# Full-array matmuls outside the projections, and projections as eight 64-by-32 tiles, in an attention and long-convolution kernel on one core

## The chip, the cores and the metric

The kernel runs on one core of a Trainium2 chip. The metric is device time in microseconds (us) of one execution. TensorE (PE) multiplies, VectorE (DVE) and ScalarE (ACT) empty PE's results out of PSUM, GpSimd (POOL) works on SBUF alone and issues the loads, SyncE (SP) issues the stores.

## What is computed

Two softmax attentions per batch and head, then a gated long convolution with its output projection:

```python
# q, k, v: (8, 8, 576, 64); p: (8, 8, 32, 64)
p_packed = sm_attn(p, k, v)              # 32 packed queries against 576 positions
out = sm_attn(q, p_packed, p_packed)     # 576 positions against the 32 packed rows
x = out.transpose(0, 2, 1, 3).reshape(8, 576, 512)
proj = x @ w_proj                        # (8, 576, 1536) -> x1, x2, x3
x2_conv = irfft(rfft(x2, axis=1) * rfft(filter_fft, axis=0), n=576, axis=1)
result = (x1 * x2_conv * x3) @ w_out     # (8, 576, 512)
```

## The kernel before

Each batch passes through four stages, each a Python generator that issues a small piece of work and then yields the time that its author counted for the piece.

- `front(b)`: transposes of k (`kTp`), p (`pTp`, function `pack`) and q (`qTp`, and `qTtp` for the last 64 positions, function `q_tail`), the first attention (`s1`, `pv`, `z1`), the transpose `ppT` of its result into the tile `ppk`, and the second scores (`score2`), which leave the softmax weights `a2n`.
- `turn(b)`: the packed rows times `w_proj` (`qp`, into `qm`), then `a2n` times the forward Fourier matrix `wc` (`fp`, `fpt`) and the transposes of `a2n` (`a2tp`).
- `middle(b)`: `spectrum` (the spectrum `f`, times the filter into `tt`, sums on POOL into `gm`) and `gate` (the products `x1` and `x3`, into `w`).
- `back(b)`: `inverse` (inverse transform `x2`, times `w` into `y`) and `project_out` (`o`, scaled into `os`, stored).

The function `together` merges four stages of four different batches: it takes each time the stage that is least far along by yielded time over its total (`STAGES`). So one round of the main loop, in full with `back(b-3)`, `middle(b-2)`, `turn(b-1)` and `front(b)`, is full for b = 4 to 7. Each engine runs its own instructions in the order that results. All 576 positions are handled as four tiles of 128 and one of 64.

PSUM is two rings of buffers: three called `pa` (all of `front` and `turn`) and five called `pm` (`middle`, `back`). A new tile waits for the reader of the tile three (or five) places earlier in its ring.

A matmul whose stationary operand has 64 columns, or whose contraction has 64 rows, runs in a smaller tiling of the PE array; rows of the profile show it as 128\*64 or 64\*128 (rows \* columns). Before, these are: the four transposes of `pack` and of `ppT` (line 218, 306), `q_tail` (257), the tail of `score2` (325), both matmuls of each projection (354), the fifth matmul of each `fp` and `fpt` group (368, 375), the fifth transpose of each `a2tp` (384), and the tail of `project_out` (460). All others are in the full tiling.

Of the kernel before, what the change touches and what calls it, by code (L numbers as in the profile page):

```python
# [11 lines left out]
FP32 = mybir.dt.float32  # L12
# [34 lines left out]
def _constants(S):  # L47
# [31 lines left out]
def kernel(  # L79
# [42 lines left out]
    wc = const.tile([P, 5, 640], FP16, tag="wc", name="wc")  # L122
# [3 lines left out]
    hri = const.tile([P, 2, 2, DM], FP32, tag="hri", name="hri")  # L126
    hni = const.tile([P, 2, DM], FP32, tag="hni", name="hni")
# [4 lines left out]
    rings = [const.tile([P, H, 2 * NPK], FP16, tag=f"ppk{r}", name=f"ppk{r}") for r in range(NR)]  # L132
    filt = [sb.tile([P, DM], FP32, tag="os", name=f"filt{i}", bufs=5) for i in range(5)]
# [6 lines left out]
    def load(b):  # L140
# [5 lines left out]
        qt = ld.tile([64, H, D], FP16, tag="qt", name=f"qt_b{b}")  # L146
# [14 lines left out]
    nc.scalar.dma_start(wc[0:64, 4, :], d_wc.ap()[0:64, 4, :])  # L161
# [11 lines left out]
    for r in range(NR):  # L173
        nc.vector.memset(pks[r][:], 0.0)
        nc.vector.memset(rings[r][:], 0.0)


    def prologue_filter():
# [5 lines left out]
        dst = [hri[:, 0, 0, :], hri[:, 1, 0, :], hri[:, 0, 1, :], hri[:, 1, 1, :], htail[:]]  # L184
# [15 lines left out]
    def front(b):  # L200
# [8 lines left out]
        qTt = sb.tile([P, H // 2, 64], FP16, tag="qTt", name=f"qTt_b{b}")  # L209
# [44 lines left out]
        def q_tail():  # L254
            tp = pst(f"qTtp_b{b}", [P, H // 2, 64], FP16)
            for g in range(H // 2):
                nc.tensor.transpose(tp[:, g, :], qt[:, 2 * g:2 * g + 2, :], ident[0:64, 0:64])
            nc.vector.tensor_copy(out=qTt[:], in_=tp[:])
# [44 lines left out]
        pT = pst(f"ppT_b{b}", [P, 2, P], FP16)  # L303
        for t in range(2):
            for u in range(2):
                nc.tensor.transpose(pT[u * D:(u + 1) * D, t, :], ppn[:, t, :], ident[:])
        for u in range(2):
            nc.vector.tensor_copy(out=R[u * D:(u + 1) * D, :, (1 - u) * NPK:(2 - u) * NPK],
                                  in_=pT[u * D:(u + 1) * D].rearrange("p t (h j) -> p (t h) j", j=NPK))
# [251 lines left out]
```

## Time and profile before

| | |
|---|---|
| median of 3 runs | 259.2 us (258.7 to 260.14) |
| the profiled execution | 259.07 us, of which 257.3 us are from its first to its last instruction |
| PE, DVE, ACT, POOL busy | 233.8, 157.8, 135.1, 136.2 us |
| mean granted PE clock | 0.979 of full |

Busy time is the time in which an engine has at least one instruction under way. On PE, matmuls overlap, so that its use is better read from the distance between starts.

### The profile page before, as it was taken

The page shows a single profiled execution, that of the slowest core. Times are in us where ns is not written, and L with a number is a line of the kernel's source. Part 1 is how long each engine was busy: PE and PEld are TensorE (multiplying, and loading weights), DVE is VectorE, ACT ScalarE, POOL GpSimd, SP SyncE. Part 2 cuts the span into 40 slices and gives each one's busy share as a digit, 9 for nine tenths or more (in the row PEclk, how much of TensorE's full clock was granted, in tenths as well). Part 3 has the DMA queues.
Part 4 walks back from the last instruction along what each step waited for, and adds up shares of the span by engine and source line. Part 5 has one row for each costly group of instructions (what it writes and reads, how often), then busy time and mean ns, then how long its engine had stood idle before and what let it go on. Part 6 is the DMA issues. An engine that isn't in the chain of part 4 may idle for free.

```text
span 257.3 us, 5269 instructions
## 1 busy us (share of the span) xinstructions
PE 233.8 (91%) x2034; PEld 137.9 (54%) x2034; DVE 157.8 (61%) x382; ACT 135.1 (53%) x267; POOL 136.2 (53%) x128
## 2 busy tenths in 40 slices
PE   0949879977998999999999999999999999999983
PEld 0327527643565566565655565566656553565541
DVE  2241445894129759954795479556966596659560
ACT  2234575460845855664656565755575465442513
POOL 8215274679114859548844784347432843463640
PEclk9998999995899999999999999999999999999999
DMA  5999999991199493978666857112002200230314
GB/s 154 247 224 202 202 198 202 195 196 16 6 175 222 66 130 46 109 119 134 135 80 79 127 150 108 43 41 89 17 3 80 83 23 1 82 104 38 129 40 167
DMA packets 36522, 28.70 MB, mean 112 GB/s; under 512 B 8080, under 2 KB 31184, under 8 KB 36496
## 3 DMA queue, kind: packets, MB, share of 16 engines
q0 software_dynamic: 29504, 16.52, 48.5%
q1 hardware_dynamic: 6336, 11.10, 12.6%
q10 hardware_dynamic: 656, 0.74, 1.0%
q8 instruction: 16, 0.26, 0.4%
q14 instruction: 10, 0.08, 0.1%
HBM read 35.42 MB, written 9.44 MB: 174 GB/s over the span
## 4 chain that ended last, share of the span: by engine, by line
PE 77%; DMA 6%; POOL 6%; ACT 5%; issue 3%; DVE 2%; POOLq 1%; ACTq 0%; DVEq 0%
PE o_b L460 12%; PE x_b L451 9%; PE fp_b L368 7%; PE x_b L424 6%; PE f_b L401 6%; DMA kn_b<-in_k_dram 6%; PE qp_b L354 6%; PE x_b L429 5%; PE pv_b L286 4%; PE s_b L238 4%; PE kTp_b L227 4%; PE qTp_b L248 3%; PE hp L190 3%; PE a2tp_b L384 2%; POOL tt_b L411 2%
## 5 line engine op out<-in xcount | busy, mean ns | idle before, releaser
L411 POOL TENSOR_TENSOR tt_b<-tt_b,tt_b 128x1024 f32<-128x1024 f32 x16 | 37.7, 2354 | 44.0 <-DVE tt_b L409 43.9
L460 PE MATMUL o_b<-wout,y_b 128*128 128x512 f16 (+1 forms) x160 | 41.3, 380 | 0.2 <-ACT x1s_b L426 0.2
L356 ACT CAST qm_b<-qp_b 128x512 f16<-128x512 f32 x48 | 27.8, 594 | 25.1 <-PE qp_b L354 24.6
L431 DVE TENSOR_TENSOR w_b<-x1s_b,x_b 128x288 f32<-128x288 f32 x64 | 28.3, 451 | 20.1 <-ACT x1s_b L426 19.5
L451 PE MATMUL x_b<-ac,gm_b 128*128 128x288 f16 x192 | 37.0, 302 | 3.8 <-POOL gm_b L415 1.7
L463 ACT ACTIVATE os_b<-o_b 128x512 f32<-128x512 f32 (+1 forms) x40 | 23.9, 597 | 30.2 <-PE o_b L460 29.9
L409 DVE TENSOR_TENSOR tt_b<-f_b,hri 128x512 f32<-128x512 f32 x48 | 31.4, 680 | 7.5 <-PE f_b L401 7.5
L426 ACT COPY x1s_b<-x_b 128x288 f32<-128x288 f32 x64 | 25.2, 397 | 16.7 <-PE x_b L424 16.3
L453 DVE SCALAR_TENSOR_TENSOR y_b<-w_b,x_b 128x288 f16<-128x288 f32 x64 | 27.3, 447 | 6.7 <-PE x_b L451 6.5
L333 POOL TENSOR_TENSOR a2n_b<-e_b,zr_b 128x512 f16<-128x512 f16 (+1 forms) x24 | 21.3, 903 | 13.2 <-DVE zr_b L332 7.7
L424 PE MATMUL x_b<-a2t_b,qm_b 128*128 128x288 f16 x128 | 27.0, 288 | 0.2 <-ACT x1s_b L426 0.2
L429 PE MATMUL x_b<-a2t_b,qm_b 128*128 128x288 f16 x128 | 26.7, 286 | 0.0
L451 PEld LDWEIGHTS <-gm_b 128*128 128x128 f16 x192 | 17.0, 102 | 15.0 <-issue 5.0
L401 PE MATMUL f_b<-qm_b,fa_b 128*128 128x512 f16 x80 | 24.3, 379 | 0.2 <-ACT x1s_b L426 0.2
L368 PE MATMUL fp_b<-wc,a2n_b 128*128 128x512 f16 (+1 forms) x80 | 21.9, 381 | 1.1 <-POOL a2n_b L333 1.1
L460 PEld LDWEIGHTS <-y_b 128*128 128x128 f16 (+1 forms) x160 | 14.1, 100 | 15.6 <-issue 4.1
L354 PE MATMUL qp_b<-wp,ppk 128*64 128x512 f16 x96 | 20.6, 405 | 0.9 <-ACT e_b L328 0.5
L240 ACT ACTIVATE e_b<-s_b 96x384 f16<-96x384 f32 x32 | 15.6, 488 | 9.3 <-PE s_b L238 8.5
L227 PE MATMUL kTp_b<-ident,kn_b 96*128 96x96 f16 x192 | 14.0, 210 | 5.2 <-DMA kn_b<-in_k_dram 3.6
L369 ACT CAST fa_b<-fp_b 128x512 f16<-128x512 f32 x16 | 9.4, 586 | 14.8 <-PE fp_b L368 14.8
L227 PEld LDWEIGHTS <-kn_b 96*128 96x128 f16 x192 | 11.1, 101 | 9.4 <-issue 4.2
L238 PEld LDWEIGHTS <-kT_b 128*96 128x96 f16 x192 | 13.7, 131 | 3.9 <-issue 0.9
(70 smaller groups left out, 380.0 us busy)
## 6 DMA issues: line engine op xcount, KB each, us to landing
out_dram<-os_b SPq DMA_DIRECT2D x32, 256.0 KB, 2.3
kn_b<-in_k_dram POOLq DMA_DIRECT2D x8, 576.0 KB, 9.7
vn_b<-in_v_dram POOLq DMA_DIRECT2D x8, 576.0 KB, 9.6
qn_b<-in_q_dram POOLq DMA_DIRECT2D x8, 512.0 KB, 10.5
wp<-in_moe_w_proj_dram POOLq DMA_DIRECT2D x3, 512.0 KB, 20.1
filt<-in_moe_filter_fft_dram SPq DMA_DIRECT2D x4, 256.0 KB, 8.4
out_dram<-os_b SPq DMA_DIRECT2D x16, 64.0 KB, 2.8
wc<-c_wc ACTq DMA_DIRECT2D x4, 160.0 KB, 6.6
```

Source lines behind the costliest of these rows:

```text
L227: nc.tensor.transpose(tp[:, hh, ii, :], kn[:, 2 * g + hh, ts(ii, P)], ident[0:KP, 0:KP])
L354: mark["project"] = nc.tensor.matmul(qp[u * D:(u + 1) * D, :], Rd[:, g, NPK:3 * NPK], wp[:, g, ts(c, DM)], start=True, stop=True)
L356: nc.scalar.copy(out=qm[:, t, ts(c, DM)], in_=qp[:])
L368: nc.tensor.matmul(fp[:], a2n[0:n, i, ts(t, P)], wc[0:n, i, 0:DM], start=(i == 0), stop=(i == 4))
L401: nc.tensor.matmul(f[:], fa[:, t, ts(m, P)], qm[:, t, ts(1, DM)], start=(t == 0), stop=(t == 1))
L409: nc.vector.tensor_tensor(out=x[:, j, :], in0=f[:], in1=h, op=ALU.mult)
L411: nc.gpsimd.tensor_tensor(out=x[:], in0=tt[r][:], in1=x[:], op=ALU.add)
L424: nc.tensor.matmul(x1[:], qm[:, t, ts(m, P)], a2t[:, t, cols], start=(t == 0), stop=(t == 1))
L429: nc.tensor.matmul(x3[:], qm[:, t, ds(2 * DM + m * P, P)], a2t[:, t, cols], start=(t == 0), stop=(t == 1))
L431: nc.vector.tensor_tensor(out=w[:, m, e, :], in0=x1s[:], in1=x3[:], op=ALU.mult)
L451: nc.tensor.matmul(x2[:], gm[:, 4 if j == 2 else 2 * e + j, ts(m, P)], ac[:, j, cols], start=(j == 0), stop=(j == 2))
L460: nc.tensor.matmul(o[0:n, :], y[:, m, COL0[i]:COL0[i] + n], wout[:, m, :], start=(m == 0), stop=(m == ND - 1))
```

## The change

Every matmul outside the projections is brought to the full tiling (the filter's prologue apart, with its ten 64-row matmuls). The two 128-row halves of p and of the packed result are transposed by one matmul in place of four, and spread by four copies of 64x128, two on ACT and two on DVE, in place of two of 64x256 on DVE. The last 64 positions are packed by head parity: head 2g in rows 0 to 63, head 2g+1 in rows 64 to 127 (tiles `a2c`, `e2c`, `qTm`). The fifth block of `wc` gets a second copy in rows 64 to 127, so that 320 KB of it are loaded in place of 80. A projection of one third of `w_proj` becomes eight matmuls of 64 rows and 32 columns with two PSUM tiles, in one piece of `turn` (three pieces, before six). The filter's three parts lie side by side in `h3`, so that one DVE instruction of 1024 elements takes the place of two of 512. Two totals in `STAGES` and some yields are other numbers.

```diff
-    wc = np.zeros((P, 5, 640), dtype=np.float16)
+    wc = np.zeros((P, 6, 640), dtype=np.float16)
     for i in range(5):
         wc[0:TILE_SZ[i], i, :] = _f16(fwd[:, TILE_T[i]].T)
+    wc[64:128, 5, :] = wc[0:64, 4, :]
...
         def pack():
-            pp = pst(f"pTp_b{b}", [P, 2, P], FP16)
+            pp = pst(f"pTp_b{b}", [P, P], FP16)
+            nc.tensor.transpose(pp[:], pn[:], ident[:])
             for t in range(2):
-                for u in range(2):
-                    nc.tensor.transpose(pp[u * D:(u + 1) * D, t, :], pn[:, t, :], ident[:])
-            for u in range(2):
-                nc.vector.tensor_copy(out=pk[u * D:(u + 1) * D, :, u * NPK:(u + 1) * NPK],
-                                      in_=pp[u * D:(u + 1) * D].rearrange("p t (h j) -> p (t h) j", j=NPK))
+                for a in range(2):
+                    cp = nc.scalar.copy if t == a else nc.vector.tensor_copy
+                    cp(out=pk[a * D:(a + 1) * D, 4 * t:4 * t + 4, a * NPK:(a + 1) * NPK],
+                       in_=pp[t * D:(t + 1) * D, :].rearrange("p (h j) -> p h j", j=NPK))
...
+        def score2_tail():
+            sp = pst(f"s2t_b{b}", [P, P])
+            for gg in range(2):
+                for u in range(2):
+                    nc.tensor.matmul(sp[:, ts(gg, 2 * NPK)], qTm[:, gg, u, :], Rd[:, 2 * u + gg, NPK:3 * NPK],
+                                     start=(u == 0), stop=(u == 1))
+            normal(sp[:], e2c[:], a2c[:], zs[:, 4, 0:4], zr[:, 4, 0:4])
...
-        def project(c, t):
-            qp = pst(f"qp_b{b}", [P, DM])
+        def project(c):
+            qp = [pst(f"qp_b{b}", [P, DM]) for u in range(2)]
+            for g in range(H // 2):
+                for u in range(2):
+                    mark["project"] = nc.tensor.matmul(
+                        qp[u][g * NPK:(g + 1) * NPK, :], R[u * D:(u + 1) * D, 4 * u + g, (1 - u) * NPK:(2 - u) * NPK],
+                        wp[u * D:(u + 1) * D, g, ts(c, DM)], start=True, stop=True)
             for u in range(2):
-                g = 2 * t + u
-                mark["project"] = nc.tensor.matmul(qp[u * D:(u + 1) * D, :], Rd[:, g, NPK:3 * NPK],
-                                                   wp[:, g, ts(c, DM)], start=True, stop=True)
-            nc.scalar.copy(out=qm[:, t, ts(c, DM)], in_=qp[:])
+                nc.scalar.copy(out=qm[:, u, ts(c, DM)], in_=qp[u][:])
...
+        def forward(o, t, cols):
+            for i in range(4):
+                nc.tensor.matmul(o, a2n[:, i, ts(t, P)], wc[:, i, cols], start=(i == 0), stop=False)
+            nc.tensor.matmul(o, a2c[:], wc[:, 4 + t, cols], start=False, stop=True)
...
-            for j in range(2):
-                h = hri[:, r, j, :] if m < 2 else (hni[:, r, :] if j == 0 else hri[:, r, 0, :])
-                nc.vector.tensor_tensor(out=x[:, j, :], in0=f[:], in1=h, op=ALU.mult)
+            h = h3[:, r, 1:3, :] if m < 2 else h3[:, r, 0:2, :]
+            nc.vector.tensor_tensor(out=x[:], in0=f[:].unsqueeze(1).broadcast_to([P, 2, DM]), in1=h, op=ALU.mult)
...
-                nc.tensor.matmul(o[0:n, :], y[:, m, COL0[i]:COL0[i] + n], wout[:, m, :],
+                nc.tensor.matmul(o[:], y[:, m, ds(COL0[i], P)], wout[:, m, :],
...
-    STAGES = ((back, 7200.0), (middle, 9400.0), (turn, 3900.0), (front, 5800.0))
+    STAGES = ((back, 7200.0), (middle, 9400.0), (turn, 4300.0), (front, 5700.0))
```

The written order of each engine's instructions shows what moves. Counted there, PE changes its tiling 241 times before and 66 times after; 17 of the 24 projections run as eight matmuls in a row, three of these 17 directly after one another at the start, and the other seven are cut in two by matmuls in the full tiling.

On PE, in the rows of a full round where the projections begin, one pair of projection matmuls before (`qp` the projection, `x` the inverse transform, `kTp` the transpose of k; between the last two rows shown stands a second load and matmul of the pair):

```order
L451 MATMUL x_b_1989<-ac,gm_b_1488 128x288
L354 LDWEIGHTS ppk_80
L354 MATMUL qp_b_1976<-wp,ppk_80 64x512
L451 LDWEIGHTS gm_b_1488
L424 LDWEIGHTS qm_b_1496
```

and after, where two PSUM tiles alternate through eight loads and eight matmuls (each of the two repeats four times):

```order
L422 MATMUL f_b_1970<-qm_b_1518,fa_b_1680 128x512
L373 LDWEIGHTS ppk_79
L373 MATMUL qp_b_1976<-wp,ppk_79 32x512
L373 MATMUL qp_b_1977<-wp,ppk_79 32x512
L232 LDWEIGHTS kn_b_1496
```

So two pieces of `turn` with one PSUM tile each became one piece with two.

On ACT, in the stretch from the projections' first copies on (`qm` is the copy of a projection, `x1s` of a gate product, `kT` of a transposed k, `e` an exponential of scores), before:

```order
L328 ACTIVATE e_b_1848<-s_b_1906 64x256
L356 CAST qm_b_1947<-qp_b_1948 128x512
L356 CAST qm_b_1947<-qp_b_1976 128x512
L426 COPY x1s_b_1997<-x_b_1994 128x288
L232 COPY kT_b_1987<-kTp_b_1980 128x576
L356 CAST qm_b_1947<-qp_b_2003 128x512
L240 ACTIVATE e_b_1952<-s_b_2007 96x2x6x32
```

and after, with the copies of the second attention's packed rows (`ppk`) ahead of them:

```order
L318 COPY ppk_79<-ppT_b_1863 64x2x2x32
L483 ACTIVATE os_b_1893<-o_b_1888 64x512
L446 COPY x1s_b_1907<-x_b_1904 128x288
L331 ACTIVATE e_b_1869<-s_b_1875 128x512
L331 ACTIVATE e2c_b_1870<-s2t_b_1942 128x128
L377 CAST qm_b_1975<-qp_b_1976 128x512
L377 CAST qm_b_1975<-qp_b_1977 128x512
L225 COPY pk_77<-pTp_b_1999 64x4x32
L446 COPY x1s_b_2039<-x_b_2036 128x288
L237 COPY kT_b_2017<-kTp_b_2010 128x576
L377 CAST qm_b_1975<-qp_b_2024 128x512
L245 ACTIVATE e_b_1988<-s_b_2045 96x2x6x32
```

Four copies (two of `ppk`, two of `pk`) are new on ACT; the second one of `ppk` stands behind `os`, the copy of the output tail, and the second one of `pk` behind `kT`.

On DVE, from the row sums of the second softmax to the first `y` of the inverse transform's second half, before:

```order
L329 TENSOR_REDUCE zs_b_1850<-e_b_1848 128x16
L332 RECIPROCAL zr_b_1851<-zs_b_1850 128x16
L385 COPY a2t_b_1656<-a2tp_b_1899 128x576
L329 TENSOR_REDUCE zs_b_1850<-e_b_1848 64x8
L385 COPY a2t_b_1656<-a2tp_b_1915 128x576
L453 SCALAR_TENSOR_TENSOR y_b_1933<-w_b_1489,x_b_1934 128x288
L409 TENSOR_TENSOR tt_b_1944<-f_b_1941,hri 128x512 x2
L230 COPY kT_b_1962<-kTp_b_1955 128x576
L220 COPY pk_78<-pTp_b_1964 64x8x32 x2
L453 SCALAR_TENSOR_TENSOR y_b_1933<-w_b_1489,x_b_1971 128x288
```

and after:

```order
L406 COPY a2t_b_1681<-a2tp_b_1897 128x576
L333 TENSOR_REDUCE zs_b_1873<-e_b_1869 128x16
L406 COPY a2t_b_1681<-a2tp_b_1922 128x576
L333 TENSOR_REDUCE zs_b_1873<-e2c_b_1870 128x4
L473 SCALAR_TENSOR_TENSOR y_b_1962<-w_b_1512,x_b_1963 128x288
L429 TENSOR_TENSOR tt_b_1973<-f_b_1970,h_72 128x1024
L235 COPY kT_b_1997<-kTp_b_1990 128x576
L225 COPY pk_77<-pTp_b_1999 64x4x32 x2
L473 SCALAR_TENSOR_TENSOR y_b_1962<-w_b_1512,x_b_2005 128x288
```

The sequence is the same but for the first copy of `a2t`, which moved ahead of the first row sum, and for the sizes: one `tt` of 1024 elements, a narrower tail sum, and `pk` copies of half the width.

## Rows read from the trace of the kernel before

**Rows 1.** The page's busy times: us, share of the span, instructions.

```profile
PE 233.8 (91%) x2034; PEld 137.9 (54%) x2034; DVE 157.8 (61%) x382; ACT 135.1 (53%) x267; POOL 136.2 (53%) x128
```

**Rows 2.** Chain that ended last, rounds b=4 and b=7: start, us, what.

```profile
110.33 0.97 PE o_b L460 x4
...
190.62 0.97 PE o_b L460 x4
```

**Rows 3.** Timeline of PE, 149 to 156 us: start, us, line, tiling, moving shape, count.

```profile
149.10 0.41 PE L424 MATMUL x_b<-a2t_b,qm_b 128*128 128x288 f16 x2
149.34 0.41 PE L429 MATMUL x_b<-a2t_b,qm_b 128*128 128x288 f16 x2
149.68 0.29 PE L257 MATMUL qTtp_b<-ident,qt_b 64*128 64x64 f16 x4
149.90 0.42 PE L424 MATMUL x_b<-a2t_b,qm_b 128*128 128x288 f16 x2
...
150.50 0.30 PE L306 MATMUL ppT_b<-ident,ppn_b 128*64 128x128 f16 x4
150.63 1.03 PE L460 MATMUL o_b<-wout,y_b 128*64 128x512 f16 x4
...
152.09 0.40 PE L322 MATMUL s_b<-ppk,qT_b 128*128 128x64 f16 x8
152.32 0.77 PE L375 MATMUL fpt_b<-wc,a2n_b 128*128 128x64 f16 x10
```

**Rows 4.** Timeline of PE, 128 to 137.5 us, the stretch of the projections.

```profile
130.38 0.30 PE L451 MATMUL x_b<-ac,gm_b 128*128 128x288 f16 x1
130.60 0.41 PE L354 MATMUL qp_b<-wp,ppk 128*64 128x512 f16 x2
130.94 0.42 PE L451 MATMUL x_b<-ac,gm_b 128*128 128x288 f16 x2
...
132.46 0.59 PE L401 MATMUL f_b<-qm_b,fa_b 128*128 128x512 f16 x2
...
134.06 0.41 PE L354 MATMUL qp_b<-wp,ppk 128*64 128x512 f16 x2
...
137.03 0.82 PE L460 MATMUL o_b<-wout,y_b 128*128 128x512 f16 x3
```

**Rows 5.** Timelines of DVE, 123 to 129 and 127 to 156 us.

```profile
126.45 0.69 DVE L329 TENSOR_REDUCE zs_b<-e_b 128x16 f32<-128x512 f16 x1 [0.16 <-ACT e_b L328]
...
131.99 0.82 DVE L453 SCALAR_TENSOR_TENSOR y_b<-w_b,x_b 128x288 f16<-128x288 f32 x2
...
135.02 0.44 DVE L453 SCALAR_TENSOR_TENSOR y_b<-w_b,x_b 128x288 f16<-128x288 f32 x1
```

**Rows 6.** Timeline of ACT, 127 to 156 us.

```profile
133.43 0.59 ACT L356 CAST qm_b<-qp_b 128x512 f16<-128x512 f32 x1 [0.65 <-PE qp_b L354]
...
151.69 0.59 ACT L463 ACTIVATE os_b<-o_b 64x512 f32<-64x512 f32 x1 [0.94 <-PE o_b L460]
```

**Rows 7.** Groups by shape: count, busy us, mean ns of one, idle before.

```profile
L409 DVE TENSOR_TENSOR tt_b<-f_b,hri 128x512 f32<-128x512 f32 x48 | 31.4, 680 | 7.5 <-PE f_b L401 7.5
L431 DVE TENSOR_TENSOR w_b<-x1s_b,x_b 128x288 f32<-128x288 f32 x64 | 28.3, 451 | 20.1 <-ACT x1s_b L426 19.5 <-PE s_b L322 0.2
L385 DVE COPY a2t_b<-a2tp_b 128x576 f16<-128x576 f16 x16 | 6.6, 416 | 0.5 <-PE a2tp_b L384 0.5
L220 DVE COPY pk<-pTp_b 64x256 f16<-64x256 f16 x16 | 4.5, 283 | 0.1
L329 DVE TENSOR_REDUCE zs_b<-e_b 64x8 f32<-64x256 f16 x8 | 3.1, 387 | 0.0
L377 ACT CAST fa_b<-fpt_b 128x256 f16<-128x256 f32 x8 | 3.0, 373 | 0.7 <-PE fpt_b L375 0.7
L354 PEld LDWEIGHTS <-ppk 128*64 128x64 f16 x96 | 6.0, 107 | 11.9 <-issue 9.8 <-DVE tt_b L409 0.2
```

**Rows 8.** Busy time by stretch; the last three columns are PE clock, DMA share, GB/s.

```profile
10.00:20.00 10.00, 6.40 (x40) 3.01 (x39) 3.45 (x7) 2.57 (x5) 1.71 (x3) 0.90 1.34 224
```

More of the change, by code (lines that the diff above doesn't have):

```diff
@@ L121 @@
     ident = const.tile([P, P], FP16, tag="ident", name="ident")
-    wc = const.tile([P, 5, 640], FP16, tag="wc", name="wc")
+    wc = const.tile([P, 6, 640], FP16, tag="wc", name="wc")
     ac = const.tile([P, NI, S], FP16, tag="ac", name="ac")
@@ L132 @@
     rings = [const.tile([P, H, 2 * NPK], FP16, tag=f"ppk{r}", name=f"ppk{r}") for r in range(NR)]
+    qTms = [const.tile([P, 2, 2, P], FP16, tag=f"qTm{r}", name=f"qTm{r}") for r in range(2)]
     filt = [sb.tile([P, DM], FP32, tag="os", name=f"filt{i}", bufs=5) for i in range(5)]
@@ L175 @@
         nc.vector.memset(rings[r][:], 0.0)
+    for r in range(2):
+        nc.vector.memset(qTms[r][:], 0.0)
     def prologue_filter():
@@ L254, in q_tail @@
         def q_tail():
[L255 to L258, printed above, removed]
+            tp = pst(f"qTtp_b{b}", [P, 2, P], FP16)
+            for gg in range(2):
+                nc.tensor.transpose(tp[:, gg, :], qt[:, 2 * gg:2 * gg + 2, :], ident[:])
+            for u in range(2):
+                c = slice(u * 64, (u + 1) * 64)
+                nc.vector.tensor_copy(out=qTm[:, :, u, c].rearrange("p g (e r) -> p g e r", e=2),
+                                      in_=tp[:, :, c].rearrange("p g (r e) -> p g e r", e=2))
         k_turn(0)
@@ L302, in front @@
         yield 150
-        pT = pst(f"ppT_b{b}", [P, 2, P], FP16)
+        pT = pst(f"ppT_b{b}", [P, P], FP16)
+        nc.tensor.transpose(pT[:], ppn[:], ident[:])
+        Rv = R.rearrange("p (u t g) c -> p u t g c", u=2, t=2)
         for t in range(2):
[L305 to L309, printed above, removed]
@@ L310, in front @@
-        yield 230
-        e2 = sb.tile([P, 5, HJ], FP16, tag="e2", name=f"e2_b{b}")
-        a2n = sb.tile([P, 5, HJ], FP16, tag="a2n", name=f"a2n_b{b}")
+            for a in range(2):
+                cp = nc.scalar.copy if t == a else nc.vector.tensor_copy
+                cp(out=Rv[a * D:(a + 1) * D, :, t, :, (1 - a) * NPK:(2 - a) * NPK],
+                   in_=pT[t * D:(t + 1) * D, :].rearrange("p (g u j) -> p u g j", g=2, u=2))
+        yield 60
+        e2 = sb.tile([P, 4, HJ], FP16, tag="e2", name=f"e2_b{b}")
@@ L316, in score2 @@
         def score2(ii):
-            n = P if ii < 2 else 64
-            w = 2 if ii < 2 else 1
             sp = pst(f"s2_b{b}", [P, 2, HJ])
-            if ii < 2:
-                for h in range(H):
-                    nc.tensor.matmul(sp[:, :, ts(h, NPK)], qT[:, h, ii, :], R[:, h, :], start=True, stop=True)
-            else:
-                for g in range(H // 2):
-                    nc.tensor.matmul(sp[0:64, 0, ts(g, 2 * NPK)], qTt[:, g, :], Rd[:, g, NPK:3 * NPK],
-                                     start=True, stop=True)
@@ L513 @@
     first = turn(0)
-    some(first, 6)
+    some(first, 3)
     def ahead():
```

80 lines of the change are left out of this document (42 added, 38 removed).

## Prediction

> **What bounds the kernel now.** I read four views in this order. The busy times come first [rows 1]: PE is busy for 91% of the span, DVE for 61%, ACT and POOL for 53%. That makes PE the candidate, but its matmuls overlap, so the next question is what the chain that ended last goes through. In the middle of the run it lies on PE, and the same four matmuls of the output projection come back at 110.33 and, three rounds later, at 190.62 [rows 2]: 80.29 / 3 = 26.76 us for a full round of four stages. I then read PE's timeline for where that round loses time. Two gate products in the full tiling start 0.24 us apart (149.10, 149.34), which is two matmuls of 288 columns at 0.12 each. The next group, in 64 rows, starts not 0.24 but 0.34 later, and the group behind it is late again: eight small matmuls take 0.23 (152.09 to 152.32), so four should take 0.115, yet 149.68 to 149.90 is 0.22 [rows 3]. So a change of tiling costs about 0.10 us in and 0.10 out. For a projection pair it is the same: one matmul of 288 columns (0.12) is followed after 0.22, and the pair holds PE for 0.34, though its two matmuls of 512 columns run side by side and would need 0.215 (four in one tiling: 150.63 to 151.59, 0.96 less 0.10 on the way out) [rows 3, 4]. A pair thus costs 0.10 + 0.34 = 0.44.
>
> The last view is DVE's timeline. From 126.45 to 135.46 (135.02 + 0.44) it runs without a pause, 9.0 us [rows 5]. In that stretch PE is not alone in setting the pace: the spectrum matmul starts at 132.46, and its PSUM buffer, five places on in the ring, was released by the first of the two `y` at 131.99 + 0.45 = 132.44. ACT is as close: the projection at 134.06 takes the place of one whose copy ran from 133.43 to 134.02 [rows 4 to 6]. In the projections' stretch the slack of PSUM is thus a few hundredths of a microsecond.
>
> **The change part by part.**
>
> Changes of tiling: 241 before and 66 after, at 0.10 in and 0.10 to 0.12 out (0.12 behind a projection). Before 241 x 0.101 = 24.4; after 66 x 0.11 = 7.0. PE saves 17.4 us in all, or 15 to 19 by the ends of these prices.
>
> Projections: before, six pairs of 0.44 per batch, 2.64. After, three groups of eight, of which about four in ten are cut in halves. No row shows eight tiles at once. The rows nearest to it are the pairs: two matmuls together take 0.41 [rows 4], so the second starts within about 0.01 of the first. Lower bound 0.44 per group (all eight side by side), upper bound 0.10 + 8 x 0.215 + 0.12 = 1.94 (one after another). I take 0.46, a pair plus six more starts at 0.003 to 0.004; a half costs 0.44. About 1.75 per batch, so 0.9 saved, of which 0.5 is already in the count of tilings.
>
> Weight loads: one load of 128\*64 takes 0.107 [rows 7]. In a pair the second load shows no time of its own; if all eight stood in a line ahead of their matmuls, a group would be 7 x 0.107 = 0.75 longer and a round 2.2. I take nothing, from the pair. The Trainium skill ("TensorE: Matmul & The Clock Gate", LDWEIGHTS) prices a load by its columns at 1.2 GHz: 53 ns for 64 columns and 27 for 32, so that eight in a line would be 0.21. The row with 107 does not agree with it; by the page the worst case is 0.6 per round in place of 2.2.
>
> Transposes: `pack` and `ppT` shrink from four matmuls in two pairs (150.50 to 150.63, 0.13) [rows 3] to one of 128 columns, about 0.055; the fifth transpose of `a2tp` doubles, 0.03 each. Net 0.1 per batch saved. So PE alone would give in a full round 2.85: 2.2 of tilings, 0.45 of projections, 0.1 to 0.2 of transposes.
>
> DVE: the run that ends at the `y` releasing the spectrum's buffer lasts 126.45 to 132.44, 6.0 us. In it one `tt` pair becomes one instruction. 512 elements take 0.680 and 288 take 0.451, 1.02 ns per element, so 1024 take 1.20 against 2 x 0.60 in the queue with overlap, up to 1.36: a gain between 0 and 0.16, I take 0.14. The tail's row sum of 256 elements takes 0.387; half of them about 0.24, gain 0.15. Two `pk` copies of 0.283 become half as wide, gain 0.14 (0 to 0.28). One copy of `a2t` (0.416, 0.33 without overlap) moves ahead of the run [rows 7]. Together 0.75, so that the run is 5.25.
>
> ACT: four new copies per batch. Twice their width takes 0.373 [rows 7]; bounds 0.1 and 0.37, taken 0.27, so 1.1 per round on an engine with half its time free. What counts is the place. The second copy of `ppk` stands behind the copy of the output tail, which starts about 1.2 after the transpose (150.50 to 151.69) and takes 0.59 [rows 3, 6]. What waits for it is the second half of `score2`'s first tile, its exponential and DVE's run: that run starts 2.95 behind the transpose in place of 2.71 (126.45 less 123.74, one round before 150.50). The second copy of `pk` stands behind `kT` and holds the PSUM buffer that the second projection wants.
>
> **The sum.** In three stretches of a full round. From `ppT` to the middle spectrum, before 132.46 - 123.74 = 8.72 [rows 3, 4], DVE's queue decides: 2.95 + 5.25 = 8.2, gain 0.5 to 0.6. PE, relieved of some 1.5 us there, waits for it. From that spectrum to the output projection (137.03), before 4.57: four pairs become one group and two halves (1.76 to 1.34), and of the 0.42 some 0.15 goes to waits for two ACT copies of 0.59 in a row, gain 0.3. From there to the next `ppT` (13.47) PE decides: three excursions less (two `fp`, `q_tail`), 0.6, but `fpt` (0.28) now comes earlier, gain 0.3. A full round gains 1.2 of the 2.85, and four of them 4.8. In the rounds b=3 and b=8 three stages share DVE and ACT, so more of PE's gain stays: 2.0 each. Round b=2: 1.5. The stretch before it waits for POOL and ACT as much as for PE: 0.8. At the start 320 KB of `wc` come in place of 80; 246 KB at the 224 GB/s that the loads reach there [rows 8] are 1.1 us, of which I charge half, 0.6, as the first k is on its way at the same time. The last two rounds: 0.4. Together 4.8 + 4.0 + 1.5 + 0.8 - 0.6 + 0.4 = 10.9. The profiled execution took 259.07 (0.1 under the median, span and 1.8 around it): 259.07 - 10.9 = 248.
>
> **The rivals.**
>
> PE stays the bound. Outside the projections' stretch DVE and ACT have idle time; if their queues catch up, the whole 2.85 comes: 4 x 2.85 + 2 x 2.6 + 2.5 + 1.5 + 0.4 = 21, so 238. Against it stands the buffer released 0.02 before it was taken [rows 4, 5].
>
> The evictions take nearly all of it. The new copies on ACT, two projection tiles at a time out of a ring of three, and `tt` at 1.36 cost the full rounds all but 0.2; with 1 us each in b=2, b=3 and b=8 that is 4, so 255. For it speaks that ACT stands as close as DVE; against it that DVE's queue loses work for certain. The Trainium skill ("TensorEngine Tiling (Array Packing)", PSUM Bottleneck) says that tiling speeds up TensorE but not the emptying of PSUM. The trace agrees in the projections' stretch and not in the other half of a round.
>
> Slower: the eight tiles run one after another. A group is 1.94, three are 5.8 against 2.64, so PE loses 3.2 per round and gains 1.95 elsewhere (2.85 less 0.9). Eight rounds lose 1.2 each, 267 to 269. It decides from a group of (2.64 + 1.95) / 3 = 1.5 us on. Against it: pairs do run side by side. That the change does nothing for tilings is ruled out by the order.
>
> **How the numbers follow.** The forecast (243 to 252) gets 0.5, PE as bound (236 to 243) 0.24, evictions taking nearly all (252 to 257.8) 0.14, the groups in a line 0.08, and 0.04 lies within 0.5%, about what a measurement here can tell from no change. So faster 0.88, same 0.04, slower 0.08. The predicted time is 248. The range, 236 to 257, takes in PE's full gain and the evictions that take nearly all, and leaves out the slower and the no-change case, 0.12 together, and some 0.05 below.
>
> **What would show it.** Right: distances of PE starts outside the projections with no 0.10 steps; groups of eight with starts a few ns apart and 0.46 in all; a full round of about 25.5; new waits of PE for DVE's `y` and `tt` and for ACT's `qm`, 0.3 to 0.8 at a time, at the projections; a POOL wait for one longer `tt`. Wrong: no such waits (round under 24.5), or ACT busy without a pause from the `ppk` copies to the last `qm` (round over 26.3), or a group near 1.5. A second stretch at half clock in the first 80 us would add some 2 us that no step here counts.

## The result and the profile after

The changed kernel takes 245.83 us (median of four runs, 244.16 to 246.51) against 259.31 us for the kernel before (four runs, 258.70 to 260.14): a ratio of 0.947 (0.941 to 0.952). It is faster by 13.5 us. The forecast was 248 and a gain of 10.9.

The profiled execution took 245.76 us, span 244.0. First the page's busy times (us, share, instructions), beside [rows 1], and the granted PE clock in 40 equal slices, in tenths:

```profile
PE 217.3 (89%) x2066; PEld 134.7 (55%) x2066; DVE 153.7 (63%) x360; ACT 138.0 (57%) x299; POOL 135.4 (55%) x128
...
PEclk9997965999989999999999999999999999999999
```

PE lost 16.5 us of busy time and the span 13.3. The chain that ended last gives the length of a round, from the same four matmuls as in [rows 2] (start, us, what):

```profile
132.64 0.86 PE o_b L480 x4
...
146.62 0.59 ACT os_b L483
147.92 0.61 ACT e_b L331
...
151.40 0.96 DVE tt_b L429
...
152.45 0.45 DVE kT_b L235
...
153.42 0.27 ACT pk L225
...
153.73 0.41 PE s_b L243 x6
...
157.22 0.86 PE o_b L480 x4
...
181.81 0.86 PE o_b L480 x4
```

A full round is 157.22 - 132.64 = 24.58, the next 24.59; before it was 26.76. It gained 2.17, not the 1.2 of the forecast. The chain now leaves PE between 146.6 and 153.7, for ACT and DVE around the second scores and the first multiply. It comes back to PE at the first scores of the next batch, which wait for the last copy of `pk`. PE has 55% of the whole chain, where it had 77%.

PE's timeline in a full round, 120 to 129.2 us (start, us, line, tiling, moving shape, count):

```profile
120.91 0.22 PE L313 MATMUL ppT_b<-ident,ppn_b 128*128 128x128 f16 x1
120.96 1.03 PE L480 MATMUL o_b<-wout,y_b 128*128 128x512 f16 x4
...
122.07 0.29 PE L449 MATMUL x_b<-a2t_b,qm_b 128*128 128x288 f16 x1
122.38 0.28 PE L342 MATMUL s_b<-ppk,qT_b 128*128 128x64 f16 x4
...
122.55 0.39 PE L405 MATMUL a2tp_b<-ident,a2n_b 128*128 128x128 f16 x4
122.95 0.28 PE L342 MATMUL s_b<-ppk,qT_b 128*128 128x64 f16 x4
...
124.67 0.59 PE L422 MATMUL f_b<-qm_b,fa_b 128*128 128x512 f16 x2
125.20 0.41 PE L373 MATMUL qp_b<-wp,ppk 64*32 64x512 f16 x8
125.55 0.43 PE L232 MATMUL kTp_b<-ident,kn_b 96*128 96x96 f16 x6
...
127.05 0.41 PE L444 MATMUL x_b<-a2t_b,qm_b 128*128 128x288 f16 x2
127.30 0.41 PE L449 MATMUL x_b<-a2t_b,qm_b 128*128 128x288 f16 x2
128.00 0.53 PE L471 MATMUL x_b<-ac,gm_b 128*128 128x288 f16 x3 [0.30 <-ACT x1s_b L446]
128.37 0.38 PE L422 MATMUL f_b<-qm_b,fa_b 128*128 128x512 f16 x1
...
129.15 0.41 PE L243 MATMUL s_b<-pk,kT_b 128*96 128x64 f16 x6
```

Three things are to be seen. The eight tiles of a projection run side by side: 0.41 from the first start to the last end, where one of them takes 422 ns in the mean of 192. The next group starts 0.35 after the eight, and with the 0.10 on the way in that is 0.45 (0.46 forecast). `ppT` is one matmul, and the output projection starts 0.05 behind it, without the step of 0.10. And there are waits. Two matmuls of 288 columns need 0.25 (127.05 to 127.30), but the inverse transform comes 0.70 behind the second pair, so PE stands still for 0.45. Twice it waits 0.2 ahead of a half of the second scores (one matmul takes 0.12: 122.07 to 122.38, and four transposes 0.21: 122.55 to 122.95).

The timelines of DVE and of ACT in that stretch, the second for the copies:

```profile
122.11 0.47 DVE L318 COPY ppk<-ppT_b 64x128 f16<-64x128 f16 x2
...
123.96 0.69 DVE L333 TENSOR_REDUCE zs_b<-e_b 128x16 f32<-128x512 f16 x1
...
126.73 1.22 DVE L429 TENSOR_TENSOR tt_b<-f_b,h 128x1024 f32<-128x1024 f32 x1
...
128.83 0.82 DVE L473 SCALAR_TENSOR_TENSOR y_b<-w_b,x_b 128x288 f16<-128x288 f32 x2
```

```profile
121.16 0.26 ACT L318 COPY ppk<-ppT_b 64x128 f16<-64x128 f16 x1
122.03 0.59 ACT L483 ACTIVATE os_b<-o_b 64x512 f32<-64x512 f32 x1 [0.60 <-PE o_b L480]
122.64 0.26 ACT L318 COPY ppk<-ppT_b 64x128 f16<-64x128 f16 x1
...
127.55 0.40 ACT L446 COPY x1s_b<-x_b 128x288 f32<-128x288 f32 x1 [0.65 <-PE x_b L444]
...
128.83 0.26 ACT L225 COPY pk<-pTp_b 64x128 f16<-64x128 f16 x1 [0.34 <-DVE pk L225]
```

DVE's run starts 3.05 behind `ppT` (123.96 - 120.91; 2.95 forecast), and its first `y` of 128.83 ends, at half of the pair's 0.82, near 129.25, so the run is 5.3 long (5.25 forecast). Yet the spectrum is at 128.37, before that `y` has even started. This is the line on which the forecast of the round fails, as told below.

Where the 13.3 us of the span came from, by the first matmul of an output projection in PE's timeline (that of batch 0 runs in round b=2, that of batch 1 in b=4, that of batch 5 in b=8):

| stretch | before | after | gain | forecast |
|---|---|---|---|---|
| start to output projection of b=2 | 66.26 | 66.42 | -0.2 | 0.2 |
| from there to that of b=4 | 44.01 | 41.20 | 2.8 | 3.5 |
| from there to that of b=8 (four full rounds) | 106.18 | 97.29 | 8.9 | 4.8 |
| from there to the end | 40.85 | 39.08 | 1.8 | 2.4 |

The full rounds gave nearly twice what was forecast, and the other stretches 1.7 less together. A second trace of the same kernel, from the run of it at the end of the experiments, has 67.86, 40.18 and 97.27 in the first three stretches, so differences of 1 us between the first two rows are within what one kernel shows. At the start a loss hides: the first transpose of the second batch's k stands at 37.89 before and at 41.29 after, 3.4 late.

### The profile page after: what moved, and what is told of

It reads as the page before. It is cut to its first block, busy times and chain, and to the rows that moved or that the text cites. A ratio compares the mean times of both kernels' runs of the same rounds, so it can differ in the third digit from the quotient of the medians.

```text
span 244.0 us, 5344 instructions
## 1 busy us (share of the span) xinstructions
PE 217.3 (89%) x2066; PEld 134.7 (55%) x2066; DVE 153.7 (63%) x360; ACT 138.0 (57%) x299; POOL 135.4 (55%) x128
## 4 chain that ended last, share of the span: by engine, by line
PE 55%; DMA 13%; DVE 13%; POOL 6%; ACT 5%; issue 5%; POOLq 1%; ACTq 0%; DVEq 0%
PE o_b L480 13%; DMA qn_b<-in_q_dram 8%; PE fp_b L386 6%; DMA vn_b<-in_v_dram 6%; PE x_b L471 5%; PE f_b L422 5%; PE pv_b L295 4%; PE x_b L449 4%; PE x_b L444 4%; PE s_b L243 3%; DVE tt_b L429 3%; PE qTp_b L253 3%; DVE zs_b L333 2%; PE qp_b L373 2%; POOL tt_b L431 2%
## 5 line engine op out<-in xcount | busy, mean ns | idle before, releaser
L429 DVE TENSOR_TENSOR tt_b<-f_b,h 128x1024 f32<-128x1024 f32 x32 | 39.1, 1220 | 10.2 <-PE f_b L422 10.0
L480 PE MATMUL o_b<-wout,y_b 128*128 128x512 f16 x160 | 41.9, 384 | 0.2 <-ACT x1s_b L446 0.2
L471 PE MATMUL x_b<-ac,gm_b 128*128 128x288 f16 x192 | 34.4, 287 | 4.5 <-POOL gm_b L438 1.7
L377 ACT CAST qm_b<-qp_b 128x512 f16<-128x512 f32 x48 | 25.9, 590 | 11.2 <-PE qp_b L373 10.8
L446 ACT COPY x1s_b<-x_b 128x288 f32<-128x288 f32 x64 | 25.2, 399 | 10.9 <-PE x_b L444 10.5
L449 PE MATMUL x_b<-a2t_b,qm_b 128*128 128x288 f16 x128 | 27.4, 286 | 0.5 <-ACT x1s_b L446 0.5
L444 PE MATMUL x_b<-a2t_b,qm_b 128*128 128x288 f16 x128 | 27.2, 286 | 0.0
L335 POOL TENSOR_TENSOR a2n_b<-e_b,zr_b 128x512 f16<-128x512 f16 x16 | 16.7, 1051 | 12.8 <-DVE zr_b L334 12.2
L480 PEld LDWEIGHTS <-y_b 128*128 128x128 f16 x160 | 15.1, 99 | 13.2 <-issue 0.6
L386 PE MATMUL fp_b<-wc,a2n_b 128*128 128x512 f16 x64 | 17.6, 393 | 2.3 <-POOL a2n_b L335 2.3
L232 PEld LDWEIGHTS <-kn_b 96*128 96x128 f16 x192 | 12.1, 103 | 9.2 <-issue 3.9
L373 PE MATMUL qp_b<-wp,ppk 64*32 64x512 f16 x192 | 15.6, 422 | 0.7 <-ACT e_b L331 0.6
```

What stands on the lines that cost most here:

```text
L232: nc.tensor.transpose(tp[:, hh, ii, :], kn[:, 2 * g + hh, ts(ii, P)], ident[0:KP, 0:KP])
L377: nc.scalar.copy(out=qm[:, u, ts(c, DM)], in_=qp[u][:])
L386: nc.tensor.matmul(o, a2n[:, i, ts(t, P)], wc[:, i, cols], start=(i == 0), stop=False)
L429: nc.vector.tensor_tensor(out=x[:], in0=f[:].unsqueeze(1).broadcast_to([P, 2, DM]), in1=h, op=ALU.mult)
L444: nc.tensor.matmul(x1[:], qm[:, t, ts(m, P)], a2t[:, t, cols], start=(t == 0), stop=(t == 1))
L449: nc.tensor.matmul(x3[:], qm[:, t, ds(2 * DM + m * P, P)], a2t[:, t, cols], start=(t == 0), stop=(t == 1))
```

## Experiments

All ratios are to the kernel before, on the same chip, with a 95% interval. The round is that of the profiled execution, from one output projection to the next, against 24.59 in the changed kernel.

**Where the round's gain comes from.** Theory A: outside the projections PE is the bound, and each group that no longer leaves the full tiling gives its whole 0.2. Rival B: evictions set the round's pace, and shorter PE work is lost to waits. The first experiment brings the 64-row matmul back in three of four groups of the forward transform, at the same place in every engine's order:

```diff
-            nc.tensor.matmul(o, a2c[:], wc[:, 4 + t, cols], start=False, stop=True)
+            r = slice(t * 64, (t + 1) * 64) if t == 0 or cols.start == 0 else slice(0, P)
+            nc.tensor.matmul(o, a2c[r, :], wc[r, 4 + t, cols], start=False, stop=True)
```

> The changed kernel, with the fifth matmul of both fp groups and of the first fpt group again on 64 rows; same operands, same results, every engine's order unchanged. Three excursions of PE to 64*128 and back per batch, 24 in all. Theory A (PE's own time sets the pace of a round outside the projections, and a change of tiling costs 0.10 us each way): each step of 0.10 is back in the starts, a full round goes from 24.59 to about 25.2, the kernel is 4 to 5 us slower than the changed one (about 250). Theory B (evictions set the round, PE has slack everywhere, the gain came from the merged multiply and from the order): the steps are there too, but a full round stays under 24.8 and the total within 1.5 us of 245.8.

It took 250.0 us (249.77 to 250.45), ratio 0.964 (0.959 to 0.969), span 248.2, and a round 25.21: 0.62 more for three excursions, 0.21 each. PE's timeline there:

```profile
135.36 1.03 PE L386 MATMUL fp_b<-wc,a2n_b 128*128 128x512 f16 x4
136.32 0.39 PE L388 MATMUL fp_b<-wc,a2c_b 64*128 64x512 f16 x1
136.64 0.60 PE L423 MATMUL f_b<-qm_b,fa_b 128*128 128x512 f16 x2
```

Four matmuls in the full tiling are followed after 0.96, the one in 64 rows after 0.32; in the changed kernel the same two distances are 0.87 and 0.21 (133.59, 134.46, 134.67). So an excursion costs 0.09 in and 0.11 out, and here all of it reaches the time: theory A holds in this half of the round for these three; the other groups there were not put back one by one. The second experiment brings two excursions back in the other half, between the second scores and the multiplies:

```diff
-            nc.tensor.transpose(tp[:, ds(COL0[4] - 64 * t, P)], a2c[:], ident[:])
+            r = slice(t * 64, (t + 1) * 64)
+            nc.tensor.transpose(tp[:, ds(COL0[4], 64)], a2c[r, :], ident[r, r])
```

> The changed kernel with the first transpose of each a2tp group again on 64 rows (two excursions of PE per batch, 16 in all), in the stretch between ppT and the middle spectrum, where PE waits in the changed kernel: 0.35 us for the copies of ppk, 0.45 for the buffer that the first filter multiply releases. Theory A (there the copies on ACT and DVE set the pace, and PE's tiling changes are absorbed by its waits): a full round grows by less than 0.1, the total by less than 1 us. Rival (each excursion costs 0.20 wherever it stands, as in the three that were put back on the other side of the round for +0.62): a full round +0.35, the total +2.8.

It took 246.33 us (245.54 to 247.93), ratio 0.950 (0.942 to 0.959), round 24.72: 0.13 more for two, between the two expectations and nearer to "absorbed". One of the two falls into a wait of PE: its pause ahead of the second half of the second scores, 0.19 in the changed kernel, is 0.03 here (four transposes of 0.21 from 124.16, the scores at 124.40). The 0.45 ahead of the inverse transform stays as it was.

**The eight tiles.** Are they themselves worth anything? Here the projections run again as pairs of 128 by 64 with two PSUM tiles at once. For that `w_proj` is loaded in another order of rows, in twelve pieces in place of three, and some instructions of PE around the projections stand in another order; the rest is as changed:

```diff
+            Rd = R.rearrange("p (g a) c -> p g (a c)", a=2)
+            for u in range(2):
+                for t in range(2):
+                    mark["project"] = nc.tensor.matmul(
+                        qp[u][t * D:(t + 1) * D, :], Rd[:, 2 * u + t, NPK:3 * NPK],
+                        wp[:, 2 * u + t, ts(c, DM)], start=True, stop=True)
```

> The changed kernel with each projection piece as four matmuls of 128 rows and 64 columns (two pairs) in place of eight of 64 by 32; w_proj is loaded in another order of rows. Theory A: a piece takes 0.10 + 0.215 + 0.34 = 0.65 of PE in place of 0.45, 0.6 per round, of which the waits that PE has at the projections absorb about half: a full round 24.8 to 25.2, total 247 to 250. Rival (the eight tiles side by side are the main gain): a round near 26, total over 254. Rival (projections don't matter, their stretch is set by DVE and ACT): a round within 0.1 of 24.59.

244.25 us (243.20 to 245.43), ratio 0.942 (0.936 to 0.948), round 24.67. PE's timeline shows the dearer group:

```profile
125.11 0.62 PE L376 MATMUL qp_b<-wp,ppk 128*64 128x512 f16 x4
125.67 0.43 PE L234 MATMUL kTp_b<-ident,kn_b 96*128 96x96 f16 x6
```

A piece holds PE for 0.56, with the way in 0.65, as expected, against 0.45; three pieces make 0.6. The round grew by 0.08 alone, less than expected. So the eight tiles are quicker and give a tenth of a microsecond per round, since the projections stand where PE waits. (The whole time is 1.6 us under the changed kernel's, though the intervals of the two ratios overlap. POOL's order at the start is another here too, see below, which would account for it; it was not separated.) The Trainium skill ("TensorEngine Tiling (Array Packing)", PSUM Bottleneck) says that tiling speeds up TensorE but not the emptying of PSUM; the 0.08 agrees with it.

**The merged multiply.** Two DVE instructions of 512 elements again in place of one of 1024:

```diff
-            nc.vector.tensor_tensor(out=x[:], in0=f[:].unsqueeze(1).broadcast_to([P, 2, DM]), in1=h, op=ALU.mult)
+            for j in range(2):
+                nc.vector.tensor_tensor(out=x[:, j, :], in0=f[:], in1=h[:, j, :], op=ALU.mult)
```

> The changed kernel with the filter multiply as two instructions of 512 elements again. Per spectrum DVE needs 2 x 0.60 = 1.2 plus the last one's tail, against 1.14 to 1.22. Theory A (a buffer that DVE's multiply releases late is what PE waits 0.45 us for once per round): that wait grows by 0.05 to 0.15, a full round 24.6 to 24.8, total 245.5 to 247.5. Rival (the merged multiply is a main part of the gain): a round over 25.0.

246.0 us (244.94 to 246.39), ratio 0.948 (0.943 to 0.953), round 24.56. The pair takes 1.28 in DVE's timeline, the single one 1.22: 0.06, not the 0.14 of the prediction, and it buys nothing. The expectation had the wait of 0.45 grow, because the multiply would release the buffer that PE waits for. It does not grow (0.70 from the second pair to the inverse transform in the changed kernel, 0.71 here), a first sign that the multiply is not what PE waits for there.

**The start.** POOL's timeline of the changed kernel, and that of the kernel before in the same place:

```profile
34.21 0.78 POOL L151 DMA_DIRECT2D vn_b<-in_v_dram  x1 [1.65 <-DMA kn_b<-in_k_dram]
36.92 0.89 POOL L152 DMA_DIRECT2D qn_b<-in_q_dram  x1 [1.94 <-DMA vn_b<-in_v_dram]
37.91 2.07 POOL L335 TENSOR_TENSOR a2n_b<-e_b,zr_b 128x512 f16<-128x512 f16 x2
```

```profile
34.03 0.77 POOL L148 DMA_DIRECT2D vn_b<-in_v_dram  x1 [1.31 <-PE qp_b L354]
34.90 2.62 POOL L333 TENSOR_TENSOR a2n_b<-e_b,zr_b 128x512 f16<-128x512 f16 x3
37.47 0.94 POOL L149 DMA_DIRECT2D qn_b<-in_q_dram  x1
```

The load of the third batch's q now stands ahead of the scaling of batch 0's weights `a2n`. It waits 1.94 until v's load has landed, and the forward transform, which PE needs next, starts at 39.03 in place of 36.01. Theory C: this order costs the 2 to 3 us. Rival D: PE's lower clock costs them. PE had stood still from 30.6 to 32.2, waiting for `ppk`, when its clock fell at 31.9. By the windows of 5 us (busy time of each engine, then clock, DMA share, GB/s) the clock from 35 to 40 us is half, 1.2 GHz, in the changed kernel, and full, 2.4 GHz, before:

```profile
35.00:40.00 5.00, 2.64 (x18) 0.45 (x13) 0.68 (x5) 2.51 (x6) 2.98 (x4) 0.50 1.45 196
```

```profile
35.00:40.00 5.00, 3.84 (x28) 1.50 (x27) 0.94 (x3) 2.54 (x5) 4.06 (x6) 1.00 1.45 196
```

The experiment moves the loads of q behind the scaling and nothing else:

```diff
-        nc.gpsimd.dma_start(qn[:], q[b, :, 0:512, :].rearrange("h (p i) d -> p h (i d)", i=4))
...
+        with tc.issue_after(behind) if behind is not None else ExitStack():
+            nc.gpsimd.dma_start(qn[:], q[b, :, 0:512, :].rearrange("h (p i) d -> p h (i d)", i=4))
...
-        load(2)
+        load(2, norm0)
```

> The changed kernel with the load of q for batch 2 issued behind the softmax scaling of batch 0 on POOL, as it was before the change; nothing else differs in the order of any engine. Theory A (at the start PE waits from 36.7 to 39.0 because POOL's scaling stands behind a DMA issue that waits for a landing, and goes to half clock from 31.9 to 42.2): the first fp starts near 36.5, the transposes of the second batch's k 2 to 3 us sooner, and 1 to 3 us of it stay at the end (243 to 245). Rival (the loads themselves bound the first 60 us, so that the delay is made up anyway): the total within 1 us of 245.8.

243.58 us (241.98 to 245.31), ratio 0.939 (0.932 to 0.946), span 241.0, round 24.59 as before. POOL and PE:

```profile
36.26 2.05 POOL L336 TENSOR_TENSOR a2n_b<-e_b,zr_b 128x512 f16<-128x512 f16 x2 [0.90 <-DVE zr_b L335]
```

```profile
37.52 1.89 PE L387 MATMUL fp_b<-wc,a2n_b 128*128 128x512 f16 x4
```

The scaling waits for DVE now, no longer for a load (the load of q follows at 38.62), and the forward transform starts 1.5 sooner (36.5 was expected); the second k's transposes start 1.7 sooner. The output projection of b=4 stands at 104.69 in place of 107.62 (108.04 in the second trace of the changed kernel), and the span is 3.0 shorter. That is more than the start's 1.5 to 1.7, and the clock is not separated from it: from 35 to 40 us it is 0.54 of full here too, but the stretch at half clock is shorter (32.7 to 39.6, in place of 31.9 to 42.2), and the changed kernel's next one (66.0 to 69.5) does not come. So the order, together with what the clock does after it, costs 2 to 3 us in these traces, as theory C has it. The medians differ by 2.25, with intervals of the two ratios that overlap; the later versions with this order bear it out.

**The copies.** PE's waits at the second scores were put down to the copies of `ppT` out of PSUM; those of `pTp` hold the first scores of the next batch. In ACT's rows above its second copy of `ppk` starts at 122.64, when `os` has ended (122.62) and also DVE's copies out of the same PSUM tile (122.58), so the row doesn't tell which held it. For `pk` the row names DVE, and so does the view of waits (3.4 us in all, in 5 waits). In the program as built, ACT's second copy out of either tile waits for DVE's copies out of it. Does it pay to have one engine make all four copies? All on ACT, and all on DVE:

```diff
-                    cp = nc.scalar.copy if t == a else nc.vector.tensor_copy
+                    cp = nc.scalar.copy
```

> The changed kernel with all four copies of ppk and all four of pk on ACT, one after another, where two of each were on DVE. Theory A (ACT's second copy comes late because it waits for DVE's copies out of the same PSUM tile; DVE's run from the row sums to the first multiply is what PE waits for): the four ppk copies are done about 1.0 after ppT in place of 2.0, both waits of PE at the second scores (0.18 and 0.17) vanish, the wait for the multiply's buffer (0.45) shrinks by 0.2 to 0.4, a full round 23.9 to 24.3, total 241 to 244. Rival (ACT is the tighter engine there, four more copies of 0.26 per round make it the bound): a round over 24.7.

```diff
-                    cp = nc.scalar.copy if t == a else nc.vector.tensor_copy
+                    cp = nc.vector.tensor_copy
```

> The changed kernel with all four copies of ppk and of pk on DVE. Theory A (DVE's run is what PE waits for in the projections' stretch): DVE gains four copies of 0.16 to 0.24 per round in that stretch, a full round 24.7 to 25.2, total 246.5 to 250. Rival (ACT's place in the queue, behind the copy of the output tail, is what delays the second scores, as the prediction had it): a round under 24.5.

On ACT 244.30 us (243.61 to 245.10), ratio 0.942 (0.935 to 0.949), round 24.43; on DVE 244.72 us (242.53 to 245.24), ratio 0.942 (0.933 to 0.951), round 24.69. The first was expected to gain 0.3 to 0.7 of the round and gained 0.16; the second came in at the lower end of the round it was expected to have, but 1.8 us under the expected total, since it starts sooner, see below. One of the two waits ahead of the second scores stays in the first: its four `ppk` copies end 1.33 behind `ppT` (1.0 expected). PE's timeline of it shows where more of the rest stays:

```profile
126.71 0.40 PE L373 MATMUL qp_b<-wp,ppk 64*32 64x512 f16 x4 [0.18 <-ACT pk L225]
```

The four `pk` copies now take 1.08 in a row on ACT (from 125.58), a projection waits behind them for its PSUM buffer, and a group of eight that was whole is cut in two. The waits have in part moved, not gone.

Both kernels start sooner than the changed one, since POOL's scaling happens to stand ahead of the load of q in them too. The next kernel puts the edit of the load on top of the copies on ACT all the same (both diffs above); its expectation overlooks that order:

> Both: all copies of ppk and pk on ACT, and the load of q for batch 2 behind the first softmax scaling on POOL. If the two gains are independent, as Theory A has it (one at the start, one in each full round), the total is that of the copies alone less 2 to 3 us, 238.5 to 241.5. Rival (the start's gain is lost again when the rounds are shorter, because the loads then bound them): no more than 1 us below the copies alone.

243.98 us (242.83 to 246.25), ratio 0.942 (0.931 to 0.954), round 24.43. POOL's order is the same as in the kernel with the copies on ACT, so nothing was left to gain.

**Putting it together.** Only `ppk` copied on ACT, with the load of q behind the scaling; and the same with all four `pk` copies on DVE:

```diff
-                cp = nc.scalar.copy if t == a else nc.vector.tensor_copy
+                cp = nc.scalar.copy
                 cp(out=Rv[a * D:(a + 1) * D, :, t, :, (1 - a) * NPK:(2 - a) * NPK],
```

> The changed kernel with the four copies of ppk on ACT (those of pk shared by ACT and DVE as in the changed kernel) and the load of q for batch 2 behind the first softmax scaling. Theory A (PE's two waits at the second scores come from the copies of ppk; the copies of all of pk on ACT were what took the gain away again at the projections): a full round 24.1 to 24.4, total 241.5 to 243.5. Rival (the projections' stretch takes whatever the second scores give back): a round of 24.4 to 24.6 and the total of the late load alone, 243 to 244.5.

```diff
-                    cp = nc.scalar.copy if t == a else nc.vector.tensor_copy
+                    cp = nc.vector.tensor_copy
                     cp(out=pk[a * D:(a + 1) * D, 4 * t:4 * t + 4, a * NPK:(a + 1) * NPK],
```

> As before, but with the four copies of pk on DVE, so that no copy waits for another engine's copy out of the same PSUM tile, and with two more projections in one piece. Theory A: the second scores don't wait, DVE has two copies more behind the first kT: a full round 24.2 to 24.6, total 242 to 244. Rival (DVE's run is the bound there): a round over 24.7.

The first took 243.01 us (242.18 to 244.14, six runs), ratio 0.938 (0.933 to 0.943), round 24.37; the second 243.14 us (242.11 to 244.57), ratio 0.938 (0.933 to 0.943), round 24.44. With them ran the changed kernel once more, to have it beside them:

> The changed kernel itself, on the same chip as the two versions above, for their difference from it: 245 to 247, a full round of 24.59.

246.12 us (245.49 to 247.08), ratio 0.950 (0.945 to 0.954), round 24.59. So the best version is 3.1 us (1.3%) under the changed kernel. The four full rounds give 1.1 of it (96.15 in place of 97.27 in the traces), the rest comes from the start. The kernel with the order alone (243.58) can't be told from it.

What does PE wait for ahead of the inverse transform (0.45 in the changed kernel)? There the multiply (126.73 + 1.22) and ACT's copy of the gate product (127.55 + 0.40) end at the same 127.95, and the row names the copy. In the kernel with the projections as pairs the two come apart. PE, ACT and DVE:

```profile
128.07 0.53 PE L474 MATMUL x_b<-ac,gm_b 128*128 128x288 f16 x3 [0.30 <-ACT x1s_b L449]
```

```profile
127.62 0.40 ACT L449 COPY x1s_b<-x_b 128x288 f32<-128x288 f32 x1 [0.84 <-PE x_b L447]
```

```profile
126.64 1.22 DVE L432 TENSOR_TENSOR tt_b<-f_b,h 128x1024 f32<-128x1024 f32 x1
```

The multiply ends at 127.86, the copy at 128.02, and the transform starts 0.05 after the copy, as it does in the changed kernel. So it is the copy. In the programs of both kernels as built, the inverse transform's tile takes the PSUM buffer of the gate product `x1` two tiles before it. PE thus waits for ACT, and ACT for PE's gate product just before. In the kernel before it was the same (ACT and PE), only shorter:

```profile
131.64 0.40 ACT L426 COPY x1s_b<-x_b 128x288 f32<-128x288 f32 x1
```

```profile
132.09 0.53 PE L451 MATMUL x_b<-ac,gm_b 128*128 128x288 f16 x3
```

There six transposes of k (0.25) stood between the gate products and the inverse transform and filled most of the time; in the changed order they stand ahead of the gate products. Where the buffers fall otherwise, it is the multiply. PE, DVE and ACT of the kernel with `ppk` on ACT and the late load:

```profile
124.45 0.41 PE L450 MATMUL x_b<-a2t_b,qm_b 128*128 128x288 f16 x2
124.94 0.53 PE L472 MATMUL x_b<-ac,gm_b 128*128 128x288 f16 x3
```

```profile
123.68 1.22 DVE L430 TENSOR_TENSOR tt_b<-f_b,h 128x1024 f32<-128x1024 f32 x1
```

```profile
124.65 0.40 ACT L447 COPY x1s_b<-x_b 128x288 f32<-128x288 f32 x1 [0.60 <-PE x_b L445]
```

Here the multiply ends at 124.90, the copy only at 125.05, and the transform starts at 124.94, in the buffer of the spectrum that the multiply has read. The wait is 0.24.

**The rings.** Four PSUM buffers for `front` and `turn` and four for `middle` and `back`, in place of three and five:

```diff
-    NA = 3
+    NA = 4
```

> The changed kernel with four PSUM buffers for front and turn and four for middle and back, in place of three and five. Theory A (in the projections' stretch PE waits for buffers of both rings: 0.13, 0.07 and 0.13 for those of the projections and transposes, 0.45 for the one that the filter multiply releases): the small waits go, waits on DVE's multiply and on y grow, a full round 24.5 to 25.1. Rival (the three buffers of front and turn are what holds the projections' stretch): a round under 24.2.

243.86 us (243.08 to 245.01), ratio 0.941 (0.935 to 0.947), round 24.32. That is 0.27 less than the changed kernel's and lies between the two expectations: both missed. Here PE does wait for the multiply, with the gate product `x3` (0.23 ahead of 127.26), whose tile takes the spectrum's buffer. So a fourth buffer in the one ring is worth somewhat more than the fifth in the other. The start is no sooner than in the changed kernel (the second k at 43.04, against 41.29 and 42.25 in that kernel's two traces), and the output projection of b=4 is at the same 107.62; the gain is in the rounds (95.65 in place of 97.27).

## Why the prediction came out as it did

**Right.** The direction and the range; that the round would still be set by PE in one half and, on the chain, by copies and multiplies on ACT and DVE in the other; the price of a change of tiling (0.09 in and 0.11 out when three were put back); the group of eight (0.45 for 0.46); the later start of DVE's run behind `ppT`, with the second copy of `ppk` behind `os` (3.05 for 2.95) and the length of that run (5.3 for 5.25). The slower rival, tiles one after another, is refuted by eight tiles in 0.41.

**The step that failed** is the first stretch of the full round: "From `ppT` to the middle spectrum ... DVE's queue decides: 2.95 + 5.25 = 8.2, gain 0.5 to 0.6". It measured 128.37 - 120.91 = 7.46, a gain of 1.26. Both terms of that sum were right, but the spectrum doesn't wait for the `y` that ends DVE's run: it starts 0.46 before that `y` does. That "its PSUM buffer, five places on in the ring, was released by the first of the two `y`" is therefore wrong. The rule behind it, that a new tile waits for the reader of the tile five places earlier, is not what the program does: as built, before and after the change, the spectrum takes the buffer of the spectrum six tiles before it, which in the kernel before its multiply had freed at 131.09. That the spectrum of [rows 4] started 0.02 after the buffer was thought to be free was a coincidence: it simply followed three matmuls of the inverse transform (three of 0.12 from 132.09 are 132.46), and these had waited for ACT's copy of the gate product (132.04). After the change the spectrum again follows that transform, and PE stands still for 0.45 ahead of it, for the same copy. DVE's run does decide a point of the round, but another one: the first scores of the next batch, which wait for the `pk` copies that end the run on DVE and ACT (129.09) and start at 129.15, 8.24 behind `ppT`. So more of PE's relief came through: 2.17 of the 2.85, not 1.2. The other two stretches gave 0.47 and 0.44, where 0.3 each was forecast. A coincidence of 0.02 us in a single row is no proof of a wait; the rival in which PE stays the bound deserved more than 0.24. The round of 24.59 lies close to the 24.5 under which the prediction would have called itself wrong.

**Terms off.** The start: 320 KB of `wc` were charged with 0.6 and cost nothing that shows, as `ppT` of batch 0 stands at 30.42 before and at 30.37 after. Instead a load on POOL's queue moved ahead of a scaling, and that, with the clock, costs 2 to 3 us; the prediction did not go into POOL's order there. The stretch at half clock that it named, but left out of its sum, did come: 31.9 to 42.2 and 66.0 to 69.5, where the kernel before has one from 59.0 to 65.8. The one DVE multiply saves 0.06, not 0.14. Two figures on the way are slips: 66 x 0.11 is 7.3, not 7.0, and 1.75 per batch goes with the three in ten projections that are cut in halves, not with four in ten; neither changes PE's gain by more than 0.13 per round. That the time came out only 2.2 us (0.9%) below the forecast is in part luck, as the errors partly cancel: the full rounds +4.1, the other stretches -1.7.

**Open.** What the parts of the change give in the stretch from `ppT` to the spectrum, 1.26 in all: `fpt` has moved out of it, and the two excursions of `a2tp` cost 0.13 when put back; the rest was not separated. How much of the start is the order on POOL and how much the half clock. And the waits that remain in a full round, about 1.1 us of PE: moving the copies or the buffers brought at most 0.27 of it back, and filling the 0.45 with the transposes of k, as before, was not tried.

## What to carry to other kernels

Count the groups that leave the full array tiling and multiply by 0.2 us, but only for those that stand where PE sets the pace; put the same excursions where PE waits for PSUM, and little of it shows (0.21 each for three in the one half of this round, 0.13 together for two in the other). Before a time is forecast from a buffer that comes free, check that the waiting instruction can't have another reason to start just then, such as the work ahead of it on its own engine, and look for a run in which the two candidates end at different times. And after any edit read the order of every queue, also of those that the edit doesn't touch: one load that slipped ahead of a scaling, with the half clock that went with it, took back 2 to 3 us of a gain of some 16.

## What the runs showed of the hardware

Eight tiles of 64 rows by 32 columns with 512 moving columns each take 0.41 us from the first start to the last end, while one takes 422 ns: all eight run at once. A change into that tiling costs 0.10 (two matmuls of 0.215 from 124.67, the eight at 125.20), as for the larger tiles. Copies by two engines out of one PSUM tile did not run side by side here: ACT's second `pk` copy starts at 128.83, after DVE's, and the program's own waits ask for that. Whether the chip could have run them side by side wasn't tried.
